# Block 0 in cycles of two score pairs and one weighed chunk, squares behind the copy of sums

## The chip, the core and the metric

The kernel runs on one core of one Trainium2 chip. The metric is the device time of one execution in microseconds; the kernel before takes 1423.59 us (median of 3 runs, 1423.08 to 1423.66).

## What is computed

One transformer block on x of 2048 rows and 512 columns, in float32: attention with 32 query heads of 16 columns that share one key head and one value head, then a gated feed-forward layer with 1792 inner columns. Cut to what matters:

```python
def _A_ref(x, wq, wk, wv, wo):        # H = 32, Dh = 16
    q = (x @ wq).reshape(B, S, H, Dh).transpose(0, 2, 1, 3)
    k = x @ wk
    v = x @ wv
    scores = einsum("bhqd,bkd->bhqk", q, k) * Dh ** -0.5
    p = softmax(scores)
    o = einsum("bhqk,bkd->bhqd", p, v)
    return o.transpose(0, 2, 1, 3).reshape(B, S, H * Dh) @ wo
def _B_ref(x, w_gate, w_up, w_down):
    return (gelu(x @ w_gate) * (x @ w_up)) @ w_down
h = x + _A_ref(layernorm(x), wq, wk, wv, wo)
out = h + _B_ref(layernorm(h), w_gate, w_up, w_down)
```

## The kernel before

The queries are cut into four blocks of 512 rows (b = 0 to 3), the heads into eight groups of four (g), the keys into 16 chunks of 128 (kc). For each block, group and chunk there are two *pairs* of heads. One call `score(n)` computes one pair, n counting the pairs through the whole kernel: two matmuls into a bank `s` (L387), and one exponential over 128 x 1024 on ScalarE from `s` into `p` (L391). One call `finish` *weighs* chunks: `weigh` (L395) multiplies the four heads' `p` with the values and adds into the bank `acc` of the group. There is one `acc`; when a group's last chunk is weighed, `evacuate` (L406) copies it to `oT` on VectorE (L408, the copy of sums), sends it to `acc_d` in memory (L412) and reads it back in another order into `oc` (`turn_out`, L421). After every second group the steps `invert` (L435), `divide`, `high` and `low` follow from the list `outs`, one entry for each call of `take_out`; empty entries delay them.

The program is a single stream: in the loops at the end of `run` the order of the instructions is written out by hand, and each engine takes its own in that order (SP's and VectorE's too, through `manual_schedule`).

Block 0 is where everything else is prepared. Its first group (n = 0 to 31) runs in the first loop. Behind it a second loop, from n = 32 to `lead` = 272 (block 0 has 256 pairs; the last 16 belong to block 1), goes in cycles, and in each cycle it does these things:

- It scores three pairs (two or three once there is no projection left). Into some of them it mixes the projection of the queries of blocks 1 to 3: `project_q` with `halves` yields tokens (half, number left, matmul), each a matmul over 64 of 128 rows (the profile shows it at L385) that shares the array with a score matmul on the other 64 rows. `count` tokens are used in a cycle, two to a pair. For each chunk c of a block there are 12 tokens on the first half and then 12 on the second; between them stands a copy of one column on VectorE, the `mark` (L208), and the first matmul of the second half waits for it. All of one chunk's tokens add into one bank `pq`, of which there is one.
- When a chunk of the projection is complete, VectorE splits it into `qh` and `ql` (L117, L118), squares `qh` into `qs` (L233), and SP stores `qh`, `ql`, `qh` into `q_d` (L238). When all four chunks of a block are there, the token REST comes: TensorE adds the squares (`pqn`, L249), VectorE takes their maximum (L254), and two steps go onto the list `after`: `factors`, four small operations on POOL (L259 to L268) two cycles later, and `bound`, which computes `m` on VectorE (L275) and stores it, four cycles later. `age` counts these cycles.
- It weighs the chunks that are ready, up to two.
- It calls `take_out`.
- It takes one step of `part_weights`. That generator prepares the weights of the feed-forward layer and of `wo`, 46 parts: four for `wo`, and then for each f = 0 to 13 the gate part, the up part and the down part. A part is a load through SP (`load_f`, L490), three parts ahead, into one of four buffers `w_raw`; on POOL a cast and a subtraction into one of two buffers `w_both` (L117, L118; the down part is first halved, L496); and a store to memory through POOL's own queue (L501, L507). The store of a part is issued at the next step. A load waits until POOL is through with the part that held its buffer before; a cast waits until the store of the part before the last has landed.

The load of the next group's queries, `load_q` (L367), is issued through SP when the third chunk of a group is scored.

The lines at the heart of the second loop:

```python
count = min(4 if ran < 2 or token[0] == 0 or done % 3 == 0 else 2, token[1] + 1)
for j in range(2 if token is None and n % 2 == 0 else 3):
    if 0 < j <= count // 2: ...   # a pair with two tokens in it
ready = [e[2] for e in pend if e[5] < n - 2][:2]
finish(ran)
if parts is not None and n % 9 != 8:
    next(parts, None)
```

Of the kernel before, what the change touches and what calls it, by code (L numbers as in the profile page):

```python
# [30 lines left out]
W2 = 3  # L31

AHEAD_W = 3

LAG = 6

# [14 lines left out]
def kernel(  # L51
# [12 lines left out]
    nc = tc.nc  # L64
# [91 lines left out]
    def run(outer, first):  # L156
# [28 lines left out]
        def project_q(b, cs, eng, col, whole=None):  # L185
            halves = whole is not None
            whole = whole if halves else cs
            tsl = slice(b * T, (b + 1) * T)
            xT_hi, xT_lo = xT[b]
            urgent = b == 0 and cs[0] == 0  # L190
            qss = []
            for c in cs:
                pq = psum1(f"pq_{b}_{c}")
                terms = [
                    (wt[:, d, c * P : (c + 1) * P], xt[:, d, :])
                    for d in range(DC)
                    for wt, xt in ((wq_hi, xT_hi), (wq_hi, xT_lo), (wq_lo, xT_hi))
                ]
                last = len(terms) - 1
                full = c in whole  # L200
                for n, (lhsT, rhs) in enumerate(terms if full else ()):
                    nc.tensor.matmul(pq, lhsT, rhs, start=(n == 0), stop=(n == last))  # L202
                    if n % 3 == 2 and (urgent or n < last):
                        yield 3
                for a in range(2) if not full else ():
                    if a:
                        mark = eb.tile([P, 1], F32, tag="qmark", bufs=2, name=f"mark_{b}_{c}")
                        nc.vector.tensor_copy(mark, pq[:, :1])  # L208
                    rows = slice(64 * a, 64 * a + 64)
                    for n, (lhsT, rhs) in enumerate(terms):  # L210
                        yield a, last - n, partial(
                            nc.tensor.matmul, pq, lhsT[rows], rhs[rows],
                            start=(a == 0 and n == 0), stop=(a == 1 and n == last),
                            skip_group_check=True,
                        )

                raw = None
                if (b, c) in HURRY:
                    raw = eb.tile([P, T], F32, tag="vT", bufs=3, name=f"pq_raw_{b}_{c}")
                    if b == 0:  # L220
                        nc.scalar.activation(raw, pq, AF.Copy)
                    else:
                        nc.vector.tensor_copy(raw, pq)
                    yield 3
                qh = eb.tile([P, T], F32R, tag="qh", bufs=2, name=f"qh_{b}_{c}")
                ql = eb.tile([P, T], F32R, tag="ql", bufs=2, name=f"ql_{b}_{c}")
                if raw is not None:
                    split(nc.vector, qh, ql, raw)
                else:

                    split(nc.vector if b == 0 and c == FIRST_Q else eng, qh, ql, pq)
                qs = eb.tile([P, T], BF16, tag="qs", bufs=DC, name=f"qs_{b}_{c}")
                (nc.gpsimd if urgent else nc.vector).tensor_tensor(  # L233
                    qs, qh.bitcast(F32), qh.bitcast(F32), op=ALU.mult
                )
                qss.append(qs)
                for r0, part in ((0, qh), (DH, ql), (2 * DH, qh)):
                    nc.sync.dma_start(  # L238
                        q_d[c * HC : (c + 1) * HC, r0 : r0 + DH, tsl].bitcast(F32),
                        part.bitcast(F32),  # L240
                    )
                if not halves and (raw is None or b == 0):
                    yield 3

            if halves:
                yield REST
            pn = psum1(f"pqn_{b}_{cs[0]}")[:H, :]
            for i, c in enumerate(cs):
                nc.tensor.matmul(  # L249
                    pn, sel[:, c, :], qss[i], start=(i == 0), stop=(i == len(cs) - 1)  # L250
                )
            qn = eb.tile([H, T], F32, tag="qn", bufs=1, name=f"qn_{b}_{cs[0]}")
            nc.vector.tensor_copy(qn, pn)
            nc.vector.tensor_reduce(q2[:, col : col + 1], qn, axis=AX.X, op=ALU.max)  # L254

            mm = eb.tile([H, 3], F32, tag="mm", bufs=2, name=f"mm_{b}_{cs[0]}")

            def factors():
                nc.gpsimd.tensor_scalar(  # L259
                    mm[:, 0:1], q2[:, col : col + 1], k2m, 1e-30, op0=ALU.mult, op1=ALU.add  # L260
                )
                nc.gpsimd.tensor_tensor(
                    mm[:, 1:2], mm[:, 0:1], power[:H, 0:1], op=ALU.pow
                )
                nc.gpsimd.tensor_scalar(
                    mm[:, 2:3], mm[:, 0:1], mm[:, 1:2], 0.5, op0=ALU.mult, op1=ALU.mult
                )
                nc.gpsimd.tensor_scalar(  # L268
                    mm[:, 1:2], mm[:, 1:2], k2m, 0.5, op0=ALU.mult, op1=ALU.mult
                )  # L270

            m = eb.tile([H, T], F32R, tag="m", bufs=2, name=f"m_{b}_{cs[0]}")

            def bound():
                nc.vector.tensor_scalar(  # L275
                    m, qn, mm[:, 1:2], mm[:, 2:3], op0=ALU.mult, op1=ALU.add
                )
                hs = slice(cs[0] * HC, (cs[-1] + 1) * HC)
                nc.sync.dma_start(q_d[hs, 3 * DH, tsl].bitcast(F32), m[hs].bitcast(F32))

            if urgent:
                yield 2
                factors()
                nc.scalar.activation(
                    m, qn, AF.Identity, bias=mm[:, 2:3], scale=mm[:, 1:2]
                )
                ms[b] = m
                return
            after.extend([[2, factors], [4, bound]])
            if not halves:  # L290
                yield 2


        after = []
        ms = {}
        q_first = project_q(0, range(FIRST_Q), nc.scalar, 0)
        q_rest = project_q(0, range(FIRST_Q, DC), nc.scalar, NB)
# [108 lines left out]
        def evacuate(b, g, acc):  # L406
# [61 lines left out]
            if last:  # L468
                last_out.extend([piece, gather])
            elif k == 1:  # L470

                outs.extend([[] for _ in range(6 if b == 0 else 1)])
                outs.extend([partial(invert, t), partial(invert, t + 1)] for t in (0, 2))
                outs.append([divide, high, low])
            if b == 0 and g == NG - 1:
# [555 lines left out]
        with tc.manual_schedule(engines={mybir.EngineType.SP, mybir.EngineType.DVE}):  # L1031
# [13 lines left out]
                    if parts is not None and n > 12 and n % 24:  # L1045
                        next(parts)

            token, ran, done = next(work) if first else None, 2, 0
            while n < lead:
                age()  # L1050
                rest = token == REST
                count = 0
                if token is not None and not rest:
                    count = min(4 if ran < 2 or token[0] == 0 or done % 3 == 0 else 2, token[1] + 1)
                    done += token[0] == 1 and token[1] + 1 == count
                for j in range(2 if token is None and n % 2 == 0 else 3):
                    if n == 2 * PER:
                        assert token is None
                        while after:
                            age()  # L1060
                        for _ in parts or ():
                            pass
                        if first:
                            check_bound(eb, k2m)
                        parts = work = None
                        early.close()
                        db = late.enter_context(tc.tile_pool(name="dense", bufs=1))
                        load_wo(0)
                    if 0 < j <= count // 2:
                        tokens = token, next(work)  # L1070
                        score(n, [(lane, step) for lane, _, step in tokens])
                        token = next(work, None)
                    else:
                        score(n)
                    n += 1
                    if n == 2 * PER + 4:
                        primed = dense(0)
                        next(primed)
                if rest:
                    token = next(work, None)  # L1080
                ready = [e[2] for e in pend if e[5] < n - 2][:2]
                if KC - 1 in ready:
                    ready = ready[: ready.index(KC - 1) + 1]
                ran = len(ready)
                finish(ran)
                if outs:
                    take_out()
                if parts is not None and n % 9 != 8:
                    next(parts, None)
            assert n == lead  # L1090
        assert not outs
# [421 lines left out]
```

## Time and profile before

| | us |
|---|---|
| median of 3 runs | 1423.59 |
| the profiled execution | 1424.32 |
| its span | 1422.6 |
| TensorE busy | 1402.0 (99%) |
| ScalarE busy | 1041.9 (73%) |
| VectorE busy | 539.4 (38%) |
| POOL busy | 202.4 (14%) |

Engines are named PE (TensorE, matmuls), PEld (its loads of weights), DVE (VectorE), ACT (ScalarE), POOL (GpSimd) and SP; a row with SPq is a transfer that SP issued. Times are counted from the start of the span. In a timeline a row gives the start, the length, the engine, the line, the operation, the tiles written and read, how many instructions were merged, and in brackets how long the engine had been idle before and what ended that. A busy PE is not PE at its peak. Rows of waits give who waited for whom, the total, the number and the longest. The granted clock is full throughout the span.

### The profile page before, as it was taken

How to read it: one execution, taken by the hardware profiler on the slowest of the kernel's cores; microseconds unless marked ns; L12 is line 12 of the kernel's file. 1: busy time of each engine (PE TensorE's matmuls, PEld its weight loads, DVE VectorE, ACT ScalarE, POOL GpSimd, SP SyncE). 2: the span in 40 equal slices, each digit the busy share in tenths (PEclk: the TensorE clock that was granted, in tenths of full speed). 3: DMA queues.
4: the chain of work that ended last, by engine and by line, in shares of the span. 5: the costliest groups of instructions: out<-in, count | busy, mean ns of one | idle time of the engine just before them, and what ended most of it. 6: DMA issues, size and time to landing. Idle time of an engine off the chain costs nothing.

```text
span 1422.6 us, 25583 instructions
## 1 busy us (share of the span) xinstructions
PE 1402.0 (99%) x10622; PEld 788.0 (55%) x10622; DVE 539.4 (38%) x974; ACT 1041.9 (73%) x1149; POOL 202.4 (14%) x286
## 2 busy tenths in 40 slices
PE   8999999999999999999999999999999999999998
PEld 7533333335555555555555555554555555557886
DVE  7412231313352342524252332413343342427665
ACT  7699999997787787777777777877778777772000
POOL 6356566621000000000000000000000000002000
PEclk9999999999999999999999999999999999999999
DMA  4567777743242242214252232223243241435551
GB/s 158 159 217 244 209 256 263 249 170 109 82 148 92 86 145 78 96 42 171 95 163 83 98 134 86 87 82 123 96 136 116 86 146 38 141 124 195 184 199 61
DMA packets 84700, 193.69 MB, mean 136 GB/s; under 512 B 9676, under 2 KB 24012, under 8 KB 84544
## 3 DMA queue, kind: packets, MB, share of 16 engines
q1 hardware_dynamic: 77208, 165.65, 35.6%
q0 software_dynamic: 7200, 26.22, 4.9%
q8 instruction: 85, 1.39, 0.4%
q14 instruction: 39, 0.32, 0.1%
q10 hardware_dynamic: 168, 0.10, 0.0%
HBM read 142.12 MB, written 49.55 MB: 135 GB/s over the span
## 4 chain that ended last, share of the span: by engine, by line
PE 88%; ACT 7%; DVE 1%; issue 1%; DMA 1%; POOL 0%; SPq 0%; ACTq 0%; DVEq 0%; POOLq 0%
PE acc L395 31%; PE s L387 19%; PE pu L906 8%; PE pg L906 8%; ACT p L391 7%; PE pd L906 5%; PE pd L583 3%; PE pd L605 3%; PE pg L605 3%; PE pu L605 3%; PE pq L385 2%; PE pp L583 2%; PE pq L202 1%; PE pp L714 1%; PE pxt L650 1%
## 5 line engine op out<-in xcount | busy, mean ns | idle before, releaser
L391 ACT ACTIVATE p<-s 128x1024 f32<-128x1024 f32 x1024 | 970.4, 1030 | 238.2 <-PE s L387 236.4
L395 PE MATMUL acc<-p,v_sb 128*32 128x512 f32 x4096 | 493.0, 598 | 0.1
L387 PE MATMUL s<-qg,kaug 50*128 50x512 f32 x1984 | 419.9, 425 | 5.5 <-ACT p L391 5.1
L387 PEld LDWEIGHTS s<-qg,kaug 50*128 50x128 f32 x1984 | 191.3, 184 | 255.0 <-ACT p L391 118.2
L395 PEld LDWEIGHTS acc<-p,v_sb 128*32 128x32 f32 x4096 | 113.1, 109 | 235.6 <-issue 231.0
L906 PE MATMUL pu<-x2h,w 64*128 64x512 f32 x672 | 212.7, 391 | 0.1
L906 PE MATMUL pg<-x2h,w 64*128 64x512 f32 x672 | 211.7, 391 | 0.9 <-DVE h L848 0.5
L906 PEld LDWEIGHTS pg<-x2h,w 64*128 64x128 f32 x672 | 116.1, 185 | 15.8 <-DVE g L780 1.1
L906 PEld LDWEIGHTS pu<-x2h,w 64*128 64x128 f32 x672 | 116.0, 185 | 14.9 <-issue 0.4
L906 PE MATMUL pg<-x2l,w 64*128 64x512 f32 x336 | 122.2, 391 | 0.0
L906 PE MATMUL pu<-x2l,w 64*128 64x512 f32 x336 | 122.1, 391 | 0.0
L127 POOL TENSOR_SCALAR rstd<-mv 128x1 f32<-128x1 f32 x16 | 3.6, 224 | 683.5 <-DVE mv L125 683.4
L783 ACT ACTIVATE ga<-ga 128x512 f32<-128x512 f32 x56 | 35.3, 634 | 89.2 <-DVE ga L778 89.2
L906 PE MATMUL pd<-w,gh 64*128 64x512 f32 x384 | 81.2, 392 | 0.0
L848 DVE TENSOR_TENSOR h<-h,pd 128x512 f32<-128x512 f32 x48 | 31.9, 685 | 115.4 <-PE pd L906 66.3
L408 DVE COPY oT<-acc 128x512 f32<-128x512 f32 x32 | 22.1, 691 | 130.8 <-PE acc L395 130.7
L435 DVE RECIPROCAL oc<-oc 128x128 f32<-128x128 f32 x64 | 56.4, 921 | 33.8 <-DMA oc<-acc_d 29.2
L1140 DVE SCALAR_TENSOR_TENSOR ga<-ga,g 128x512 f32<-128x512 f32 x70 | 48.3, 691 | 52.8 <-ACT ga L783 51.8
L767 DVE COPY g<-pg 128x512 f32<-128x512 f32 x56 | 38.7, 692 | 62.4 <-PE pg L906 56.7
L906 PEld LDWEIGHTS pg<-x2l,w 64*128 64x128 f32 x336 | 58.0, 185 | 7.0
L906 PEld LDWEIGHTS pu<-x2l,w 64*128 64x128 f32 x336 | 58.0, 185 | 7.0
L780 DVE TENSOR_TENSOR g<-g,pu 128x512 f32<-128x512 f32 x56 | 38.2, 683 | 40.6 <-PE pu L906 30.6
(257 smaller groups left out, 1442.2 us busy)
## 6 DMA issues: line engine op xcount, KB each, us to landing
w<-w_d SPq DMA_DIRECT2D x112, 512.0 KB
w<-w_d SPq DMA_DIRECT2D x28, 1024.0 KB
qg<-q_d SPq DMA_DIRECT2D x48, 200.0 KB
q_d<-qh SPq DMA_DIRECT2D x32, 256.0 KB
acc_d<-oT SPq DMA_DIRECT2D x31, 256.0 KB
oc<-acc_d SPq DMA_DIRECT2D x124, 64.0 KB
w_d<-w_0b POOLq DMA_DIRECT2D x14, 512.0 KB, 5.6
w_d<-w_1b POOLq DMA_DIRECT2D x14, 512.0 KB, 6.0
```

The costliest lines, as they stand in the source:

```text
L387: nc.tensor.matmul(s[:, a, :], kaug[rows, kc * P : (kc + 1) * P], qg[rows, 2 * u + a, :], start=True, stop=True,)
L391: nc.scalar.activation(p[:, 2 * u : 2 * u + 2, :], s, AF.Exp, scale=SCALE)
L395: nc.tensor.matmul(acc[32 * j : 32 * j + 32, :], v_sb[:, kc, :], p[:, j, :], start=(kc == 0), stop=(kc == KC - 1), skip_group_check=True,)
L435: nc.vector.reciprocal(oc[:, 1, sl], oc[:, 1, sl])
L583: nc.tensor.matmul(banks[k], lhsT[rows], rhs[rows], start=(turn == 0 and i == 0), stop=(turn == 1 and i == n - 1), skip_group_check=True,)
L605: nc.tensor.matmul(bank, lhsT, rhs, start=(i == 0), stop=(i == len(ts) - 1))
L767: nc.vector.tensor_copy(g, pg)
L780: nc.vector.tensor_tensor(g, g, pu, op=ALU.mult)
L783: nc.scalar.activation(a, a, AF.Tanh, scale=GELU_A * GELU_C)
L848: nc.vector.tensor_tensor(hs[t], hs[t], pd, op=ALU.add)
L906: nc.tensor.matmul(e["bank"], lhsT[rows], rhs[rows], start=i == 0 and not e["both"], stop=last and e["both"], skip_group_check=True,)
L1140: (soon or lazy).pop(0)()
```

## The change

In the second loop, a cycle now always scores two pairs and weighs one chunk (as soon as more than two are pending). The number of tokens follows a counter: `left` starts at 240, the number of tokens that come through this loop, and a cycle takes four while `left` is above `LAST_Q - n`, else two. With two, the second pair of the cycle holds them. `take_out` is called in every second cycle, and four empty entries stand ahead of the inversions instead of six. A part of the weights is taken in the cycles whose n is not a multiple of 6. The squares of the projection no longer stand directly behind the split: they are kept in the list `squares` and run in the same cycle behind `finish`, so behind a copy of sums. The step to n = 2 * PER and the start of the dense work are moved out of the inner loop.

```diff
+LAST_Q = 240
...
-                (nc.gpsimd if urgent else nc.vector).tensor_tensor(
-                    qs, qh.bitcast(F32), qh.bitcast(F32), op=ALU.mult
-                )
+                square = partial(
+                    (nc.gpsimd if urgent else nc.vector).tensor_tensor,
+                    qs, qh.bitcast(F32), qh.bitcast(F32), op=ALU.mult,
+                )
+                if full:
+                    square()
+                else:
+                    squares.append(square)
...
-                outs.extend([[] for _ in range(6 if b == 0 else 1)])
+                outs.extend([[] for _ in range(4 if b == 0 else 1)])
...
-            token, ran, done = next(work) if first else None, 2, 0
+            token, left = next(work) if first else None, 6 * (NB * DC - 2 - DC) * DC
...
-                    count = min(4 if ran < 2 or token[0] == 0 or done % 3 == 0 else 2, token[1] + 1)
-                    done += token[0] == 1 and token[1] + 1 == count
-                for j in range(2 if token is None and n % 2 == 0 else 3):
+                    count = min(4 if left > LAST_Q - n else 2, token[1] + 1)
+                    left -= count
...
-                    if 0 < j <= count // 2:
+                for j in range(2):
+                    if j >= 2 - count // 2:
...
-                ready = [e[2] for e in pend if e[5] < n - 2][:2]
-                if KC - 1 in ready:
-                    ready = ready[: ready.index(KC - 1) + 1]
-                ran = len(ready)
-                finish(ran)
-                if outs:
+                if len(pend) > 2:
+                    finish(1)
+                while squares:
+                    squares.pop(0)()
+                if outs and n % 4 == 0:
                     take_out()
-                if parts is not None and n % 9 != 8:
+                if parts is not None and n % 6:
                     next(parts, None)
```

More of the change, by code (lines that the diff above doesn't have):

```diff
@@ L291, in project_q @@
                 yield 2
-        after = []
+        after, squares = [], []
         ms = {}
@@ L1053, in run @@
                 if token is not None and not rest:
-                    count = min(4 if ran < 2 or token[0] == 0 or done % 3 == 0 else 2, token[1] + 1)
-                    done += token[0] == 1 and token[1] + 1 == count
-                for j in range(2 if token is None and n % 2 == 0 else 3):
[L1057 to L1068, printed above, removed]
-                    if 0 < j <= count // 2:
+                    count = min(4 if left > LAST_Q - n else 2, token[1] + 1)
+                    left -= count
+                if n == 2 * PER:
+                    assert token is None
+                    while after:
+                        age()
+                    for _ in parts or ():
+                        pass
+                    if first:
+                        check_bound(eb, k2m)
+                    parts = work = None
+                    early.close()
+                    db = late.enter_context(tc.tile_pool(name="dense", bufs=1))
+                    load_wo(0)
+                for j in range(2):
+                    if j >= 2 - count // 2:
                         tokens = token, next(work)
@@ L1075, in run @@
                     n += 1
-                    if n == 2 * PER + 4:
-                        primed = dense(0)
-                        next(primed)
+                if n == 2 * PER + 4:
+                    primed = dense(0)
+                    next(primed)
                 if rest:
                     token = next(work, None)
-                ready = [e[2] for e in pend if e[5] < n - 2][:2]
-                if KC - 1 in ready:
-                    ready = ready[: ready.index(KC - 1) + 1]
-                ran = len(ready)
-                finish(ran)
-                if outs:
+                if len(pend) > 2:
[3 more added lines that the diff above has]
+                if outs and n % 4 == 0:
                     take_out()
-                if parts is not None and n % 9 != 8:
+                if parts is not None and n % 6:
                     next(parts, None)
```

## The prediction

> **What bounds the kernel now.** I read the page's chain of waits first, then ScalarE's groups over block 0 behind its first group (84.8 to 325.4 us), then the timeline.
>
> ```profile
> PE 88%; ACT 7%; DVE 1%; issue 1%; DMA 1%; POOL 0%; SPq 0%; ACTq 0%; DVEq 0%; POOLq 0%
> L391 ACT ACTIVATE p<-s 128x1024 f32<-128x1024 f32 x242 | 225.9, 1047 | 15.6 <-PE s L387 15.5
> 84.81 0.50 PE L387 MATMUL s<-qg,kaug 50*128 50x512 f32 x2
> 157.58 0.72 PE L387 MATMUL s<-qg,kaug 50*128 50x512 f32 x3
> 158.14 0.39 PE L387 MATMUL s<-qg,kaug 50*128 50x512 f32 x1
> 158.38 0.39 PE L387 MATMUL s<-qg,kaug 50*128 50x512 f32 x1
> 158.18 5.61 ACT L391 ACTIVATE p<-s 128x1024 f32<-128x1024 f32 x6 [0.41 <-PE s L387]
> 158.93 1.07 PE L395 MATMUL acc<-p,v_sb 128*32 128x512 f32 x8
> 159.93 0.73 PE L387 MATMUL s<-qg,kaug 50*128 50x512 f32 x3
> 161.75 1.92 PE L395 MATMUL acc<-p,v_sb 128*32 128x512 f32 x16
> 163.60 0.72 PE L387 MATMUL s<-qg,kaug 50*128 50x512 f32 x3
> 325.57 0.73 PE L583 MATMUL pp<-wo,o_hi 64*128 64x512 f32 x4 [0.24 <-issue]
> ```
>
> TensorE and ScalarE share the bound here. Two old cycles (six pairs, three chunks) run from 157.58 to 163.60, 6.02 us, or 2.007 per chunk of two pairs. ScalarE needs 5.61 for its six exponentials and idles 0.41, because the double weighing (161.75 to 163.60) holds back the scores. All such idling sums to 15.6 us: that is the most a better rhythm can win. The 240 pairs from n = 32 to n = 272 (n counts pairs of scores) take 325.57 - 84.81 = 240.8 us.
>
> **The new cycle.** The old one with four projection halves in it takes 158.93 - 157.58 = 1.35 us for its scores and 159.93 - 158.93 = 1.00 for one chunk. A slot of scores is 0.24 (158.14 to 158.38). Two pairs with two halves have two slots fewer, two pairs with four halves one. So a cycle with two halves costs 1.35 - 0.46 + 1.00 = 1.89, with four 2.12. Without projection, the end of block 0 already runs the new form:
>
> ```profile
> 312.00 1.07 PE L395 MATMUL acc<-p,v_sb 128*32 128x512 f32 x8
> 313.00 0.73 PE L387 MATMUL s<-qg,kaug 50*128 50x512 f32 x4
> 314.80 0.73 PE L387 MATMUL s<-qg,kaug 50*128 50x512 f32 x4
> 309.93 16.67 ACT L391 ACTIVATE p<-s 128x1024 f32<-128x1024 f32 x18
> ```
>
> There 313.00 to 314.80 is 1.80, and 16.67 / 18 x 2 = 1.85 for ScalarE, which doesn't idle; I take 1.84. By its counter the change gives four halves to the first 16 cycles (n = 32 to 64), two to the next 88 (to 240), none to the last 16. Unhindered: 16 x 2.12 + 88 x 1.89 + 16 x 1.84 = 33.9 + 166.3 + 29.4 = 229.6. I add 2 us, because a finished projection bank must now be copied off behind one weighing: some eight times a quarter of a microsecond. That is 231.6, so 9 us less than 240.8. Could the two-half cycle cost more? Its bounds are 1.84 (ScalarE) and 2.12 (four halves): 4 us less, 20 more.
>
> Edits at no cost: the squares, 0.68 us each, only go behind the copy of sums on VectorE, whose idle time covers them; four empty steps instead of six and `take_out` at every second cycle put the inversion 20 pairs behind the end of a group instead of 21.
>
> **What the change adds: a faster queue of weights on POOL.** The line with `n % 6` issues a weight part in two cycles of three as before, but cycles have two pairs and not three: one part per 3 pairs instead of 4.5. POOL must do each part:
>
> ```profile
> 89.82 0.60 POOL L117 CAST w_0b<-w_0r 128x512 fp32r<-128x512 f32 x1 [2.96 <-DMA wo_d<-wo2b]
> 194.36 0.63 POOL L507 DMA_DIRECT2D w_d<-w26b  x1 [0.30 <-POOL w26b L118]
> 195.00 0.62 POOL L117 CAST w_0b<-w_0r 128x512 fp32r<-128x512 f32 x1
> 197.91 0.60 POOL L117 CAST w_1b<-w_1r 128x512 fp32r<-128x512 f32 x1
> 200.78 1.51 POOL L496 TENSOR_SCALAR w27r<-w27r 128x512 f32<-128x512 f32 x1
> 204.63 0.63 POOL L507 DMA_DIRECT2D w_d<-w27b  x1 [0.30 <-POOL w27b L118]
> 225.53 0.26 POOL L259 TENSOR_SCALAR mm<-q,k2m 32x1 f32<-32x1 f32 x1
> 227.19 0.77 DVE L275 TENSOR_SCALAR m<-qn,mm 32x512 fp32r<-32x512 f32 x1 [7.81 <-POOL mm L268]
> 92.69 0.16 DVE L208 COPY mark<-pq 128x1 f32<-128x1 f32 x1 [3.40 <-PE s L387]
> 273.26 1.30 POOL L118 TENSOR_TENSOR w212b<-w212r,w212b 128x512 fp32r<-128x512 f32 x1
> ```
>
> One triple (gate, up, down of one f) without waits is 195.00 to 205.26 = 10.26 us on POOL. The new issue rate is a triple per nine pairs, 9 x 0.945 = 8.5 us: POOL can't follow, whatever else happens.
>
> POOL executes in the order of the program, and the four small `factors` of block 2 stand in that queue. In the old program they stand behind the gate part of f = 9, and even so VectorE sat 7.81 us at `m` waiting for them (227.19). In the new program, by the order that the build gives, they stand behind the arithmetic of w212, the down part of f = 12: eleven parts more. On VectorE `m` of block 2 is followed by the `mark` copy of projection (3, 0), and TensorE's first matmul of its second half, in the second pair of the cycle that begins at n = 156, waits for that mark. Behind that matmul in TensorE's queue stand all scores and weighings, so ScalarE runs dry too; behind `m` on VectorE stand the mark, the inversions and the next copy of sums. Earlier stalls of TensorE (the factors of block 1 stand behind f = 2 in the same way) are covered by this one, because POOL doesn't wait for TensorE.
>
> When does TensorE get there? 84.81 + 33.9 + 46.5 x 1.89 + 1 = 207.6. When is POOL through w212? It starts its first triple at 89.82 as before. Lower bound: 13 triples x 10.26, less the last issue and its gap (0.93), plus one earlier group of factors (1.7): 89.82 + 133.4 - 0.9 + 1.7 = 224.0. Upper bound: the old time of the same instruction, 273.26 + 1.30 = 274.6. Between them lie POOL's waits:
>
> ```profile
> POOL w_0b L117 <- DMA w_0r<-in_B_w_gate_dram: 10.8, 2, 7.7
> POOL w25r L496 <- DMA w25r<-in_B_w_down_dram: 5.0, 1, 5.0
> POOL w23r L496 <- DMA w23r<-in_B_w_down_dram: 2.6, 1, 2.6
> POOL w_1b L117 <- DMA w_1r<-in_B_w_up_dram: 2.3, 1, 2.3
> POOL w_0b L117 <- DMA w_d<-w_1b: 9.8, 4, 3.9
> DMA to landing us min/median/max: 3.2/5.6/10.2
> SPq L490 <- POOL w_0b L118: 13.8, 6, 3.5
> ```
>
> Waits for loads (7.7 + 5.0 + 2.6 + 2.3 = 17.6 up to w212) should go: the loads now stand earlier in SP's queue, and SP issues each as soon as POOL frees its buffer, three parts ahead; the last row shows SP at that already. Waits for stores (the fifth row and its like, some 29 us) stay while the DMA engines are as busy. That gives 274.6 - 17.6 = 257. While TensorE stands still, from 208 on, its own traffic stops and stores should land nearer the 3.2 than the 5.6 of the landing row; I take 9 us off and use 248, about the middle of the bounds.
>
> The Trainium skill (DMA: Bandwidth & Descriptors, Anatomy of one DMA — SWDGE (gpsimd) path) puts such a transfer at 2.0 us plus its bytes at 436 GB/s: for the 512 KB of a store an estimate of 3.2 us. That is the trace's minimum, 3.2, but its median is 5.6; by the page no store would be waited for (the tightest reuse has 197.91 - 194.36 = 3.55 us), and the sum would be the low end, 1434.
>
> From the end of w212: factors and gap 1.76 (225.43 to 227.19), `m` 0.5, mark 0.2, and 0.3 to the matmul: TensorE resumes at 248 + 2.8 = 250.8, a stall of 43 us. Then 83 pairs x 0.945 + 29.4 + 1 = 108.8, so the phase ends at 359.6. Against 325.57 that is +34.0. The profiled execution took 1424.32 (span 1422.6; the median of the runs, 0.7 lower, is 1423.59): 1424.3 + 34.0 = **1458**. At the bounds: 224.0 gives 335.6, 1434; 274.6 gives 386.2, 1485.
>
> **Rivals.**
>
> 1. *The rhythm without the stall*: 231.6 instead of 240.8, 1424.3 - 9.2 = 1415. For it: the ScalarE idling is real, and in the old run a 7.81 us wait at `m` passed without harm, since the mark stood ahead of it there. Against it: TensorE would have to find the mark at 207.6, and POOL's bare instructions already add up to 224.0 + 2.8. Chance 0.08.
>
> 2. *SP's queue decides, not VectorE*: the loads of weights wait for POOL, and the load of `qg` for group 5 stands behind load w211, which needs the up part of f = 10 finished, seven parts before w212.
>
> ```profile
> SPq L421 <- DMA acc_d<-oT: 36.7, 8, 7.6
> 194.74 2.06 SPq L421 DMA_DIRECT2D oc<-acc_d  x4
> 197.53 0.80 SPq L367 DMA_DIRECT2D qg<-q_d  x2
> ```
>
> At 3.6 to 4 us a part that is 248 - 27 = 221, plus 4.6 for the copy of sums to land, 2.1 and 0.8 to issue, some 3 to land: 231.5. Needed at n = 160, it would leave 80 x 0.945 + 29.4 + 1 = 106: an end at 337.5, +12, 1436. This stall happens in my forecast too, but is covered by the longer one; alone it decides only if the wait at `m` does not reach TensorE. Chance 0.07.
>
> 3. *TensorE becomes the bound without a stall*: with 112 changes between row halves and column groups instead of 75, a two-half cycle costs 2.12; from 2.00 a cycle on the change is a loss. 1415 + 20 = 1435. Chance 0.03.
>
> 4. *The rhythm moves nothing*, because ScalarE finds a new wait as long as the old: 1424. Chance 0.02.
>
> **How the numbers follow.** The forecast has 0.80. Its own range is 1434 to 1485, and rivals 2 and 3 fall at its low edge; I leave out the last 7 us on top, where POOL would be as slow as with its old load waits, and take 1432 to 1478. What is left out is rivals 1 and 4 and a tail, together under 0.2. Within 0.2% (2.8 us) is about what a measurement of this kernel can't tell from no change. Faster: rival 1, 0.08. Same: rival 4, 0.02. Slower: 0.90.
>
> **What would show it.** Right: in the timeline a gap of TensorE of tens of microseconds around 208 to 250, ended by `mark` behind `m`, `m` ended by POOL's `mm`; ScalarE idle at the same place; POOL's triples at 10.3 to 12.5 us with few load waits; two-half cycles 1.89 apart before and after; everything behind block 0 as before. Wrong: no gap and `m` not waiting (rival 1), a gap ended by a DMA into `qg` (2), cycles near 2.1 (3). A gap of the right kind with another length means that POOL's pace, not the chain, was mis-sized.

## The result and the profile after

The changed kernel takes 1479.28 us (median of 6 runs, 1478.19 to 1482.14), the kernel before in the same session 1423.48: a ratio of 1.0393, 95% interval 1.038 to 1.0407. The prediction had the direction and the place, 1458 us and a range up to 1478; the time lies just above that range. The profiled execution of the changed kernel took 1478.19 us, 53.9 more than that of before. Line numbers of the code around the change have moved by seven: exponentials are L398 now, scores L394, weighings L402, `m` L282.

The page of the changed kernel, three lines of it: the span, the granted clock by slices, and the chain of waits.

```profile
span 1476.5 us, 25577 instructions
...
PEclk9998986899999999999999999999999999999999
...
PE 78%; DMA 10%; POOL 5%; ACT 3%; issue 2%; DVE 1%; SPq 1%; POOLq 0%; DVEq 0%; ACTq 0%
```

TensorE's share of the chain fell from 88% to 78%; DMA (10%) and POOL (5%) took it, and the clock digits below 9 lie in the first fifth of the span, block 0. The timeline of ScalarE there (start, time, group, in brackets the idle time before it and what ended that):

```profile
135.97 1.94 ACT L398 ACTIVATE p<-s 128x1024 f32<-128x1024 f32 x2 [9.38 <-PE s L394]
...
202.29 1.94 ACT L398 ACTIVATE p<-s 128x1024 f32<-128x1024 f32 x2 [9.18 <-PE s L394]
...
266.07 1.03 ACT L398 ACTIVATE p<-s 128x1024 f32<-128x1024 f32 x1 [33.86 <-PE s L394]
268.72 1.94 ACT L398 ACTIVATE p<-s 128x1024 f32<-128x1024 f32 x2 [1.62 <-PE s L394]
271.77 9.27 ACT L398 ACTIVATE p<-s 128x1024 f32<-128x1024 f32 x10 [1.11 <-PE s L394]
281.28 22.80 ACT L398 ACTIVATE p<-s 128x1024 f32<-128x1024 f32 x24 [0.23 <-PE s L394]
304.35 22.76 ACT L398 ACTIVATE p<-s 128x1024 f32<-128x1024 f32 x24 [0.28 <-PE s L394]
```

Three stalls, 9.4, 9.2 and 33.9 us. The first begins like the last, one block earlier: VectorE waits 12.76 us at `m` of block 1 for POOL's factors, and TensorE for the copy of sums behind it. The second is ended by the DMA that reads `qg` of group 4. Between stalls the rhythm is good: from 281.28 to 304.35 twelve two-half cycles take 23.07 us, 1.92 each on average, and ScalarE idles 0.28. TensorE's weighings show how these twelve are made up: eleven are 1.89 us apart, as the first two rows here, and one follows after 2.24, where a finished projection bank is copied off.

```profile
298.62 1.06 PE L402 MATMUL acc<-p,v_sb 128*32 128x512 f32 x8
300.51 1.07 PE L402 MATMUL acc<-p,v_sb 128*32 128x512 f32 x8
302.75 1.06 PE L402 MATMUL acc<-p,v_sb 128*32 128x512 f32 x8
```

Who ends the long stall is read from VectorE, POOL and TensorE in the timeline, in that order:

```profile
239.99 1.76 DVE L442 RECIPROCAL oc<-oc 128x128 f32<-128x128 f32 x2 [18.46 <-DMA oc<-acc_d]
263.91 0.78 DVE L282 TENSOR_SCALAR m<-qn,mm 32x512 fp32r<-32x512 f32 x1 [22.16 <-POOL mm L275]
264.62 0.13 DVE L210 COPY mark<-pq 128x1 f32<-128x1 f32 x1
...
260.90 1.26 POOL L120 TENSOR_TENSOR w212b<-w212r,w212b 128x512 fp32r<-128x512 f32 x1
...
264.81 0.79 PE L392 MATMUL pq<-xT_hi,wq_hi 64*128 64x512 f32 x1 [33.72 <-DVE mark L210]
...
379.13 0.73 PE L590 MATMUL pp<-wo,o_hi 64*128 64x512 f32 x4 [0.25 <-DMA qg<-q_d]
```

POOL ends w212 at 262.16, computes the factors, `m` waits 22.16 us for them, the mark follows, and TensorE goes on at 264.81 after 33.72 us. VectorE had already waited 18.46 us for the `oc` rows: a second late thing, hidden in the same stall. The first matmul of the dense stage, the projection of the heads' outputs, comes at 379.13 in place of 325.57, 53.56 us later, which is the loss of the whole execution to within 0.3 us. Behind block 0 next to nothing is gained or lost.

### The profile page after: what moved, and what is told of

Its sections match the earlier page's. It is cut to its first block, busy times and chain, and to the rows that moved or that the text cites. A ratio compares the mean times of both kernels' runs of the same rounds, so it can differ in the third digit from the quotient of the medians.

```text
span 1476.5 us, 25577 instructions
## 1 busy us (share of the span) xinstructions
PE 1407.0 (95%) x10622; PEld 778.5 (53%) x10622; DVE 542.4 (37%) x974; ACT 1045.6 (71%) x1149; POOL 200.5 (14%) x286
## 4 chain that ended last, share of the span: by engine, by line
PE 78%; DMA 10%; POOL 5%; ACT 3%; issue 2%; DVE 1%; SPq 1%; POOLq 0%; DVEq 0%; ACTq 0%
PE acc L402 26%; PE s L394 16%; PE pu L913 8%; PE pg L913 7%; PE pd L913 4%; PE pd L590 3%; PE pd L612 3%; PE pg L612 3%; PE pu L612 3%; ACT p L398 2%; DMA w_d<-w_0b 2%; PE pp L590 2%; DMA w_d<-w_1b 1%; POOL w_1b L120 1%; PE pp L721 1%
## 5 line engine op out<-in xcount | busy, mean ns | idle before, releaser
L398 ACT ACTIVATE p<-s 128x1024 f32<-128x1024 f32 x1024 | 974.1, 1029 | 288.4 <-PE s L394 286.7
L402 PE MATMUL acc<-p,v_sb 128*32 128x512 f32 x4096 | 500.9, 602 | 8.9 <-DVE oT L415 8.9
L394 PE MATMUL s<-qg,kaug 50*128 50x512 f32 x1984 | 423.6, 429 | 11.8 <-DMA qg<-q_d 8.1
L394 PEld LDWEIGHTS s<-qg,kaug 50*128 50x128 f32 x1984 | 192.8, 185 | 267.6 <-ACT p L398 157.8
L402 PEld LDWEIGHTS acc<-p,v_sb 128*32 128x32 f32 x4096 | 107.9, 109 | 235.5 <-issue 221.5
L392 PE MATMUL pq<-xT_hi,wq_hi 64*128 64x512 f32 x80 | 33.6, 419 | 34.6 <-DVE mark L210 33.7
```

The costliest lines, as they stand in the source:

```text
L392: step()
L394: nc.tensor.matmul(s[:, a, :], kaug[rows, kc * P : (kc + 1) * P], qg[rows, 2 * u + a, :], start=True, stop=True,)
L398: nc.scalar.activation(p[:, 2 * u : 2 * u + 2, :], s, AF.Exp, scale=SCALE)
L402: nc.tensor.matmul(acc[32 * j : 32 * j + 32, :], v_sb[:, kc, :], p[:, j, :], start=(kc == 0), stop=(kc == KC - 1), skip_group_check=True,)
```

## Experiments

Theory A: the faster issue of weight parts is the loss, because the factors that VectorE waits for stand behind them on POOL. The rivals: SP's queue by itself, or the new cycles. Every comparison is with runs of the kernel before in the same session (1423.2 to 1423.9 us).

**The old rate of parts in the new cycles.**

```diff
-                if parts is not None and n % 6:
+                if parts is not None and n % 18 in (0, 4, 10, 14):
```

> The changed kernel with one weight part per 4.5 pairs again (4 cycles of 9 issue one) and all else as changed. Theory A (the faster issue of parts on GpSimd's queue is the whole loss, and the cycles themselves gain): POOL has about 13.0 us for a triple of parts against 10.26 us of work, so its waits and the stalls of 9.4, 9.2 and 33.9 us at ScalarE's L394 rows go; left are the gain of the cycles (6.02 us per 6 pairs before, 1.92 x 3 = 5.76 now) less the four-half cycles, 1410 to 1422 us, granted clock back at 0.999. Theory B (SP's queue, where the reads of oc and qg stand behind loads, with the copies of sums once in four pairs): 15 to 25 us of stalls stay, 1435 to 1445 us. Theory C (the cycles themselves, or the lower granted clock, cost): above 1445 us.

Measured: 1427.32 us, ratio 1.0023 (1.0012 to 1.0034). Of the 55.8 us, 52 are gone, so B (1435 to 1445) and C (above 1445) fall, but A's band (up to 1422) was missed by 5 us. VectorE and ScalarE of this run, in the timeline:

```profile
213.61 0.77 DVE L282 TENSOR_SCALAR m<-qn,mm 32x512 fp32r<-32x512 f32 x1 [11.64 <-POOL mm L275]
...
215.76 1.02 ACT L398 ACTIVATE p<-s 128x1024 f32<-128x1024 f32 x1 [4.77 <-PE s L394]
```

The same wait is left in small: even at one part per 4.5 pairs POOL is behind, and the new order lets `m` hold TensorE, which the old order did not.

**The new rate in the old cycles** (the kernel before, nothing else changed).

```diff
-                if parts is not None and n % 9 != 8:
+                if parts is not None:
```

> The kernel before with its own cycles, squares and copies, only with a weight part at every cycle (one per 3 pairs, 3.01 us, in place of one per 4.5). Theory A (the rate alone): POOL needs 10.26 us for a triple that now comes in 9.03 us, so m of block 2 waits as in the changed kernel, and the time is 1450 to 1480 us. Theory C (the new cycles are needed for the loss): 1419 to 1432 us.

Measured: 1471.07 us, ratio 1.0335 (1.0314 to 1.0355). The old cycles lose 47.5 us to the rate alone. ScalarE's timeline in this run shows two stalls of the same kind, and VectorE's that `m` waits for POOL ahead of each (a third stall, 12.2 us at 241.6, follows a wait of VectorE for the `oc` rows):

```profile
165.42 1.94 ACT L391 ACTIVATE p<-s 128x1024 f32<-128x1024 f32 x2 [15.50 <-PE s L387]
...
277.39 1.94 ACT L391 ACTIVATE p<-s 128x1024 f32<-128x1024 f32 x2 [16.64 <-PE s L387]
...
158.88 0.53 DVE L275 TENSOR_SCALAR m<-qn,mm 32x512 fp32r<-32x512 f32 x1 [23.77 <-POOL mm L268]
...
274.21 0.53 DVE L275 TENSOR_SCALAR m<-qn,mm 32x512 fp32r<-32x512 f32 x1 [26.13 <-POOL mm L268]
```

**No factors of blocks 1 to 3 behind POOL's parts**, at the new rate. Their bounds are made from one set, computed from block 0's sums early on; a bound only shifts the exponent of a row, so the result stays the same but for rounding.

```diff
+            def all_factors():
+                factors()
+                shared = eb.tile([H, 4], F32, name="shared")
+                x = shared[:, 3:4]
+                nc.gpsimd.tensor_tensor(x, q2[:, 0:1], q2[:, NB : NB + 1], op=ALU.add)
+                factors(shared[:, :3], x)
+                ms["shared"] = shared
...
-            after.extend([[2, factors], [4, bound]])
+            after.extend([[2, (lambda: None) if b else all_factors], [4, bound]])
```

> The changed kernel with its rate of parts, but the factors of blocks 1 to 3 are not computed: their bounds use one set worked out from block 0, so that no m of VectorE waits for GpSimd (the bound is then a looser one, and each row's result is the same but for rounding). Theory A (the factors behind GpSimd's parts end the wait last): the stall of 33.9 us is cut to where the next late thing, the oc rows that VectorE's reciprocal waited for until 239.99, lets it: about 24 us less, and the 9.4 us at 136 go: 1440 to 1460 us. Theory B (SP's reads decide by themselves): 1468 to 1480 us. Theory C (cycles or clock): 1477 to 1482 us, the stall stays.

Measured: 1455.53 us, ratio 1.0226 (1.0205 to 1.0246): 24 us less than the changed kernel, as A had it. ScalarE's two large gaps, who ended them, and POOL, in the timeline of this run, with one row of SP's waits behind them:

```profile
200.54 1.94 ACT L414 ACTIVATE p<-s 128x1024 f32<-128x1024 f32 x2 [16.03 <-PE s L410]
...
241.97 1.02 ACT L414 ACTIVATE p<-s 128x1024 f32<-128x1024 f32 x1 [11.53 <-PE s L410]
...
196.66 0.76 PE L410 MATMUL s<-qg,kaug 50*128 50x512 f32 x1 [12.73 <-DMA qg<-q_d]
...
237.78 1.76 DVE L458 RECIPROCAL oc<-oc 128x128 f32<-128x128 f32 x2 [18.03 <-DMA oc<-acc_d]
239.47 1.12 DVE L282 TENSOR_SCALAR m<-qn,shared 32x512 fp32r<-32x512 f32 x1
...
260.73 1.28 POOL L120 TENSOR_TENSOR w212b<-w212r,w212b 128x512 fp32r<-128x512 f32 x1
...
SPq L513 <- POOL w_1b L120: 21.7, 7, 6.6
```

`m` waits for POOL no more. What stays is SP's queue, in which the reads of `qg` (gap at 200.54) and of `oc` (VectorE until 237.78) stand behind loads that wait for POOL's buffers, 21.7 us for the up parts' alone (last row). POOL's row says something else: POOL ends w212 at 262.01, against 262.16 in the changed kernel, though ScalarE's gap there was 11.5 us and not 33.9. POOL's pace did not depend on the length of TensorE's pause.

**Both edits together**: the old rate and the shared factors.

> Both earlier edits on the changed kernel: a weight part per 4.5 pairs, and the bounds of blocks 1 to 3 from block 0's factors, so that no m waits for GpSimd. With the rate alone the phase still had one stall, at L398's exps after 210 us (4.77, 1.62 and 1.35 us, m waiting 11.64 us for POOL's mm). Theory A (what is left of the loss is that same wait, and the cycles gain some 3.5 us): the stall goes, 7 us less, 1418 to 1422 us, faster than the kernel before. Rival (the new cycles themselves gain nothing): 1423 to 1427 us.

Measured: 1421.29 us (11 runs), ratio 0.9983 (0.9974 to 0.9992). This version beats both kernels, the one before by some 2 us, with an interval that leaves out 1 by little. No gap over 1.1 us is left in ScalarE's timeline over block 0, and the dense stage's first matmul stands here:

```profile
84.77 0.49 PE L410 MATMUL s<-qg,kaug 50*128 50x512 f32 x1
...
321.82 0.72 PE L606 MATMUL pp<-wo,o_hi 64*128 64x512 f32 x4 [0.24 <-DMA qg<-q_d]
```

So the phase without stalls takes 237.1 us, against 240.8 before: the rhythm itself is worth 3.7 us between the two profiled executions, 2.3 by the medians.

**A slower rate, the factors as they were**: a part per 5 pairs.

```diff
-                if parts is not None and n % 6:
+                if parts is not None and n % 10 in (0, 4):
```

> The changed kernel with a weight part per 5 pairs (cycles at n % 10 of 0 or 4) and the factors as they were. Theory A: POOL gets 14.4 us for a triple of parts, the factors of block 2 stand behind one part less, and the stall of 4.77 us shrinks to 0 to 3 us: 1419 to 1424 us. Rival (parts that come at a slower rate are late for n = 256, where all that are left are issued at once): above 1427 us.

Measured: 1422.65 us (11 runs, 1420.11 to 1427.06), ratio 0.9996 (0.9985 to 1.0007). No different from the kernel before by this measurement; theory A's band. In its profiled execution `m` of block 2 still waits 3.71 us for POOL, but ScalarE's largest gap in the phase is 1.51 us, and the phase takes 237.2 us with the factors in place.

**The squares back in their place**, on the version with both edits.

```diff
-                if full:
+                if True:
                     square()
```

> The version with both edits (rate and shared factors), and the squares of blocks 1 to 3 back where they were before, right behind the split of qh and ql and ahead of the copy of sums on VectorE. Theory A (VectorE is a third busy and the copy is waited for by the first weighing of a group, so 0.94 us can come in once per four chunks at most): 0 to 4 us above the version with both edits. Rival (the order on VectorE is what makes the cycles work): over 5 us above it.

Measured: 1421.87 us, ratio to the kernel before 0.9994 (0.9981 to 1.0006), 0.6 us above the version with both edits. Moving the squares costs and gains nothing that can be told.

**What sets POOL's pace.** The prediction had POOL through w212 at 248, by a discount on store waits. Five runs, all at the new rate, look at what those waits are. First a third `w_both` buffer, with loads two parts ahead and one `vT` less to make room, then with loads three ahead and one `vT` and one `m` less:

```diff
-                both = pw.tile([P, 2, D], F32R, tag="w_both", bufs=2, name=f"{name}b")
+                both = pw.tile([P, 2, D], F32R, tag="w_both", bufs=3, name=f"{name}b")
```

> The changed kernel with its rate of parts, and three w_both buffers in place of two, so that a part's subtraction waits for the store of three parts back; for the room, loads go two parts ahead in place of three and vT has two buffers in place of three. Theory A with POOL slowed by its stores: the store waits (1 to 5 us each) go, POOL is through w212 between 224 and 240 us in place of 262, and the time is 1432 to 1458 us. Rival (the stores only take the blame, POOL's own work or the transfers' rate is the bound): POOL through w212 after 250 us, 1465 to 1485 us.

> The changed kernel with three w_both buffers and loads still three parts ahead (room comes from vT with two buffers and m with one). The earlier run with three buffers had loads only two ahead, and POOL waited some 39 us for loads in place of stores. Theory L (a store's landing time against two buffers sets POOL's pace, whatever the rate): store waits go, loads come in time, POOL is through w212 by 224 to 238 us in place of 262, 1432 to 1455 us. Theory D (the transfers together move no more than some 240 GB/s): POOL waits for loads or stores as long as before, w212 after 252 us, 1465 to 1482 us.

Then half the bytes (the down parts in the same way; the low half is left out, and the dense stage uses the high half in its place), with two buffers and with three:

```diff
-                    w1_d[2 * f + k].bitcast(F32),
-                    both.rearrange("p i (c n) -> p i c n", c=DC).bitcast(F32),
+                    w1_d[2 * f + k][:, :1].bitcast(F32),
+                    both[:, :1].rearrange("p i (c n) -> p i c n", c=DC).bitcast(F32),
```

> The changed kernel at its rate of parts, storing the high half of each gate, up and down part alone (256 KB in place of 512 KB; the low half is left out, and the dense stage uses the high half twice, so the products are less exact). With three buffers POOL waited for loads as long as it had waited for stores, and the transfers moved 215 to 261 GB/s from 60 to 262 us in every kernel so far. Theory D (the transfers' rate, some 240 GB/s, sets POOL's pace): a third of a part's bytes is gone, POOL is bound by its own 10.26 us per triple and is through w212 by 225 to 238 us in place of 262; VectorE's oc rows end the wait, and the time is 1425 to 1455 us. Rival (a store's own latency sets it, whatever its size): POOL through w212 after 250 us, 1465 us or more.

> Both at once: the high half alone of each gate, up and down part is stored (the low half is left out, the high one is used twice), and w_both has three buffers with loads three ahead. Half stores alone took POOL through w212 at 248 us with two buffers, at 163 to 209 GB/s. Theory L: the buffers alone already did it, so this run is within 5 us of the one with three full buffers. Theory D: only with fewer bytes do three buffers help; w212 by 222 to 235 us and at least 10 us below the run with three full buffers. What stays of the stall in either case is SP's: the oc and qg reads behind the loads.

And the other half (`[:, 1:]` in place of `[:, :1]`), whose store has to wait for the subtraction:

> As the run with half stores and two buffers (changed kernel, rate of parts as changed, 256 KB stored per gate, up and down part), but the half that is stored is the low one, which POOL's subtraction writes last; the high half is left out and the low one is used in its place, so the products mean nothing. Storing the high half let POOL issue each store right behind the subtraction, without the 0.30 us that it otherwise waits for it: 0.30 x 39 = 11.7 us of the 14 us by which w212 was earlier (248.15 against 262.16). Theory G (the gap was it, and bytes matter little, since POOL still waited 41.0 us against 41.6): POOL through w212 at 256 to 262 us, 1468 to 1480 us. Theory D (the bytes were it): 246 to 251 us, 1460 to 1467 us.

Measured: 1480.04 us with three buffers and loads two ahead, 1466.12 with three and three, 1463.75 with half stores (the high half), 1457.85 with half stores and three buffers, 1471.47 with the low half. POOL's last arithmetic on w212, one row from each timeline in the same order:

```profile
261.29 1.26 POOL L120 TENSOR_TENSOR w212b<-w212r,w212b 128x512 fp32r<-128x512 f32 x1
```

```profile
249.76 1.26 POOL L120 TENSOR_TENSOR w212b<-w212r,w212b 128x512 fp32r<-128x512 f32 x1
```

```profile
246.89 1.26 POOL L120 TENSOR_TENSOR w212b<-w212r,w212b 128x512 fp32r<-128x512 f32 x1
```

```profile
242.71 1.26 POOL L120 TENSOR_TENSOR w212b<-w212r,w212b 128x512 fp32r<-128x512 f32 x1
```

```profile
255.77 1.26 POOL L120 TENSOR_TENSOR w212b<-w212r,w212b 128x512 fp32r<-128x512 f32 x1
```

- Three buffers, loads two ahead: the store waits went, and waits for loads came in their place (below, POOL's longest waits in that run: total, times, longest). No time was won: the rival's band.

```profile
POOL w_0b L119 <- DMA w_0r<-in_B_w_gate_dram: 15.1, 5, 10.1
POOL w211r L503 <- DMA w211r<-in_B_w_down_dram: 9.9, 1, 9.9
```

- Three buffers, loads three ahead: w212 ends at 251.0, 11 us earlier, 13 us less time. Neither theory's band for w212 (L up to 238, D from 252); the time lies in D's. POOL now waits for loads again, and the waits of SP, which issues them, suggest why: in its queue the reads of `oc` wait for the copies of sums, and the copies for VectorE.

```profile
POOL w_1b L119 <- DMA w_1r<-in_B_w_up_dram: 14.1, 2, 10.9
...
SPq L428 <- DMA acc_d<-oT: 22.6, 5, 6.1
...
SPq L419 <- DVE oT L415: 10.8, 1, 10.8
```

- Half the bytes: with the high half w212 ends at 248.15, between the two bands, as does the time, 1463.75; with the low half at 257.03. The high half is written by the cast, so its store does not wait the 0.30 us behind the subtraction, 39 times: 11.7 us, of which 8.9 show at w212. Against the changed kernel's 262.16 the low half gains 5.1 us: that is what the bytes were worth. Theory G's band held (1471.47 us), and theory D, that the bytes set the pace, fell with it. With three buffers on top, w212 ends at 244.0, 7 us before the run with three full buffers, and the time is 8.3 us lower: again in neither band (within 5 us for L, at least 10 for D), and the missing 0.30 us gaps are in it.

The transfers' rate can be read from the windows of 86 to 262 us (POOL's busy time, granted clock, share of the DMA engines, GB/s), first the changed kernel, then the low half:

```profile
86.00:262.00 176.00, 118.32 (x134) 0.86 0.73 238
```

```profile
86.00:262.00 176.00, 123.32 (x143) 0.86 0.63 185
```

At 185 GB/s in place of 238 POOL is busy 123 of 176 us in place of 118: it stands nearly as long. The DMA groups of the two runs from 60 to 262 us (bytes of one, median us from issue to landing), in the same order:

```profile
w_d<-w_0b POOLq DMA_DIRECT2D x13, 512.0 KB, 6.8
w_d<-w_1b POOLq DMA_DIRECT2D x13, 512.0 KB, 4.8
```

```profile
w_d<-w_0b POOLq DMA_DIRECT2D x14, 256.0 KB, 5.6
w_d<-w_1b POOLq DMA_DIRECT2D x13, 256.0 KB, 4.7
```

Half the bytes shorten a store by 0.1 to 1.2 us. With two buffers a store of 5 to 7 us is waited for at either size, since POOL, unhindered, comes back to the buffer after 3.5 us (down parts) or 5 us (gate and up parts). Why most stores take so much longer than the fastest (2.9 us in both kernels) wasn't found.

**LAST_Q at 252**, on the version with both edits.

```diff
-LAST_Q = 240
+LAST_Q = 252
```

> The version with both edits (a part per 4.5 pairs, bounds from block 0's factors) and LAST_Q at 252 in place of 240: six cycles of four halves and six with none become twelve with two. Theory A (2.12 + 1.84 against 2 x 1.92): 6 x 0.12 = 0.7 us less, 1419 to 1422 us, still faster than the kernel before. Rival (the projections of block 3 then end so close to n = 256 that what stands behind them, its bound and qg, is late): 1423 to 1430 us.

Measured: 1436.36 us, ratio 1.0093 (1.0076 to 1.011), above both bands: the rival's direction, 6 us beyond its band. The dense stage begins on time (321.61), and the loss comes right behind. The timeline suggests why, though no run tested it: the projections end later, and the loads for the dense stage are issued just ahead of a copy of sums (311.5 and 313.4 us; 301.2 and 309.6 in the version with both edits). SP then waits 13.7 us for that copy to land, in place of 7.0, and what stands behind it is late. SP's longest wait from 300 to 340 us, and ScalarE's largest gap:

```profile
SPq L444 <- DMA acc_d<-oT: 13.7, 1, 13.7
```

```profile
337.80 1.94 ACT L414 ACTIVATE p<-s 128x1024 f32<-128x1024 f32 x2 [8.56 <-PE s L410]
```

## Why the prediction was too low

**Right: what happens.** The chain was as told: POOL's parts, factors, `m`, mark, TensorE. Its two ends were tested: without the rate 52 of 55.8 us go, and with the rate alone the old kernel loses 47.5. Bare POOL work was right too. All store waits of the changed kernel between 86 and 262 us sum to 41.6, of which 2.8 lie ahead of the first triple; 262.16 less 38.8 is 223.4, against the lower bound of 224.0. The load waits vanished, as told.

**Wrong: "I take 9 us off and use 248".** The step supposed that stores land faster while TensorE stands still. The waits left in the forecast were some 33 us before that discount and 24 after it; the store waits alone were 38.8. Two rows of windows (POOL's busy time, granted clock, share of the DMA engines, GB/s) show the changed kernel ahead of the pause and in it:

```profile
89.00:231.00 142.00, 97.09 (x111) 0.93 0.72 236
231.00:262.00 31.00, 20.85 (x23) 0.53 0.77 243
```

The transfers moved as much while TensorE stood still as before, and 7.5 us of the store waits fall in these 31 us, about the same share as ahead of them (31.3 in 142). The run with shared factors shows the same 262 with a third of the pause. So the discount had no ground. The mis-sized term is POOL's waits up to w212: 14 of the 19.5 us by which the phase ended later than forecast (379.1 against 359.6).

The discount is 9 of these 14 us. The other 5 lie in the sum ahead of it, 274.6 - 17.6 = 257, which took the load waits off one for one and left the store waits at their old 29. One place shows how a wait that goes uncovers another. In the kernel before, POOL waited 7.66 us for a load, and meanwhile the store of w20, 8.5 us from issue to landing, came down unnoticed; in the changed kernel the load is there, and POOL waits 4.99 us for the same store (8.4 us). First before, then after:

```profile
108.56 0.60 POOL L117 CAST w_0b<-w_0r 128x512 fp32r<-128x512 f32 x1 [7.66 <-DMA w_0r<-in_B_w_gate_dram]
...
109.54 0.60 POOL L119 CAST w_1b<-w_1r 128x512 fp32r<-128x512 f32 x1 [4.99 <-DMA w_d<-w20b]
```

The low end of the range, where no store is waited for, was far off. The 3.2 us that the forecast leaned on is the minimum of the gate parts' stores in the kernel before; the median of the changed kernel's is 6.8.

**Right: "a cycle with two halves costs 1.89"**, and 2.12 with four: TensorE's weighings are 1.89 and 2.13 us apart. **Too small: the 2 us for copying off banks, and the 108.8 us after the stall.** From resumption to the dense stage it took 379.13 - 264.81 = 114.3, 5.5 more. Some 2.7 are the two gaps behind the stall (1.62 and 1.11 us); four cycles with a copy or with the sum of squares, each 0.3 to 0.35 us longer, are 1.4 where the forecast had 1; the rest, some 2.4, was not told apart. The stall-free version shows the same: 237.1 us for a phase that was put at 231.6. By the distances between its weighings a dozen of its cycles are longer, by 0.3 to 0.7 us, an estimated 4.7 in all in place of 2; what else is missing was not told apart. Rival 1, the rhythm without the stall, was thus priced at 1415 where 1421 is measured.

**Right: "earlier stalls are covered".** TensorE stopped at 231 and not at 207.6, because of 9.4 and 9.2 us of earlier stalls and some 5 us of longer cycles; the resumption was POOL's all the same.

**Rival 2, SP's queue**, does not decide while the factors are late, but with them out of the way it alone leaves 1455 us, where it was priced at 1436. The forecast looked at group 5's `qg` only; the largest gap (16.0 us at 200.5) is that of group 4, and the one at 242 comes from `oc` on VectorE's way to the mark. Rival 3 is refuted by the 1.89, rival 4 by the result.

## What to carry to other kernels

A counter that issues work once per cycle changes its rate when the cycle changes its length: compare the new interval with what the in-order engine behind it needs, waits included, and look for small latency-bound work queued behind the bulk. Cost a queue's waits from the trace as they are, without a discount for the calm of a stall; and when a wait goes, look for the one that ran beneath it. When a wait is lifted by a buffer, name the queue that feeds it: here the wait went from stores to loads.

## What the hardware showed unasked

After the pause of 33.7 us TensorE's matmuls were slower for some 6 us: the eight matmuls of a weighing took 1.93 us just behind the pause, and 1.06 from 271.75 on. From the changed kernel's timeline:

```profile
265.96 1.93 PE L402 MATMUL acc<-p,v_sb 128*32 128x512 f32 x8
...
271.75 1.06 PE L402 MATMUL acc<-p,v_sb 128*32 128x512 f32 x8
```

The digits 8 and 6 in the clock line are the pauses and these stretches behind them; the slow matmuls are part of the 2.7 us above. The Trainium skill (TensorE: Matmul & The Clock Gate, What's actually happening) says that the array's clock halves after an idle window of about 3.4 us and returns after a busy window of as long. The trace agrees in kind: slow matmuls follow each of the three pauses; the return took some 4 to 6 us here, and the factor for these weighings is 1.8.
